# A fused convolution and feed-forward kernel on one core: five of the convolution's six sums moved from VectorE to accumulating transfers on GpSimd's queue

## The chip, the cores and the metric

The kernel runs on 1 core of one Trainium2 chip. The metric is the device time of one execution in microseconds (us), the median of several runs. The engines are named as the profile names them: PE is TensorE's matmul, PEld its weight load, DVE is VectorE, ACT is ScalarE, POOL is GpSimd, SP is SyncE; SPq and POOLq are the queues on which SP and POOL issue transfers. All durations below are from the profiler's record of one execution.

## The reference

A softmax over seven weights per position and head gives a causal convolution over the last seven positions, whose output goes through a two-layer network with a squared ReLU. The sizes are B = 8, S = 4096, D = 192, H = 8 heads, K = 7 taps, FF = 2048.

```python
w = np.exp(weight_gen - max over taps); w = w / (w.sum(-1, keepdims=True) + 1e-9)
x_unf = x_pad[:, idx, :].reshape(B, S, K, H, D // H)      # the last 7 positions
x = np.einsum('bshk,bskhg->bshg', w, x_unf).reshape(B * S, D)
r = np.maximum(x @ w_in, 0.0)
out = (r * r) @ w_out                                     # all float32
```

## The kernel before, in words

The 32768 rows lie as 256 rows on each of 128 partitions, and are worked through in 64 chunks of 512 rows (`TC = 4` rows on each partition, numbered `c` = 0 to 63). Each chunk goes through three stages.

**Convolution** (`conv_steps`): on DVE the softmax of the weights (six steps, lines 195 to 200, with one exponential on ACT), then for each of the seven taps a product `pr` of the input rows and the tap's weights (`mul(k)`, line 211, 128 x 768 floats), and six sums of products (`add(k)`, line 216). The sum goes through `turn` (line 270: a transpose in 32 x 32 blocks on DVE, then six transfers over a DRAM scratch `xd` on SP's queue into `xT`), and `split` (lines 235, 236) makes a high and a low part of it, `xh` on ACT and `xl` on DVE. Chunks 0 and 1 are turned on PE instead and have their own order of taps, which the change doesn't touch.

**First product** (`mm1`, line 300): eight steps `j` for each chunk; each makes two blocks `ph` of 128 of the 2048 hidden rows, with 18 matmuls. ACT then takes ReLU (`rg`, line 316), square (line 320) and a rounded high part `gh` (line 324); DVE takes the low part `gl = rg - gh` (line 328).

**Second product** (`mm2_turned`, line 372): 20 matmuls for each step, which read `gh` and `gl`. PE's order of work is written out: in step `j` of a chunk `mm1` of this step stands first and behind it `mm2` of the step that lies two steps back (`LAG = 2`). At the end of a chunk `sum_turned` (lines 380 to 383) and `store_turned` (lines 391 to 405) bring the output out, the latter with 24 small transfers and one large one on SP's queue. The input of two chunks is loaded together (`load_group`, lines 91 and 92), every second chunk.

The order on each engine is the order in which the program is written out (`manual_schedule`); the framework adds only the waits. The convolution of chunk `c + 2` is spread evenly over eight steps, from step 3 of chunk `c` to step 2 of chunk `c + 1`, by `spread`: element `i` of a list of `n` is put at step `3 + 8 * i // n`. Chunk 2 is an exception: its taps are spread over steps 0 to 3 of chunk 1. What is planned for a step stands on DVE behind the `gl` of the step before:

```python
for fb in fbs: relu(c, fb)
for fb in fbs: square(c, fb)
for f in late: f()                  # gl of the step before
if done is not None: sum_turned(done)
for f in todo.pop((c, j), []): f()  # the steps of the convolution
```

In the texts below "step 6" is `j` = 6, and the products, sums and transfers of a chunk bear the number of their tap: mul4 makes the product of tap 4. The buffers `pr` come from a pool; a product takes a buffer that the sum before has set free.

Of the kernel before, what the change touches and what calls it, by code (L numbers as in the profile page):

```python
# [8 lines left out]
F32 = mybir.dt.float32  # L9
# [3 lines left out]
ALU = mybir.AluOpType  # L13
# [6 lines left out]
def kernel(  # L20
# [9 lines left out]
    nc = tc.nc  # L30
    B, S, D = x.shape
    H, K = wg.shape[2], wg.shape[3]
    G = D // H
    FF = w_in.shape[1]
    P = 128
# [4 lines left out]
    TC = 4  # L40
# [19 lines left out]
    att = ctx.enter_context(tc.tile_pool(name="att", bufs=1))  # L60
# [121 lines left out]
    def conv_steps(c, on_pe):  # L182
        gi, lo = divmod(c, CPG)
        lo *= TC
        xt, wt = x_tiles[gi], w_tiles[gi]
        n = TC * H
        wf = wt[:, lo:lo + TC].rearrange("p t h k -> p (t h) k")
        mx = att.tile([P, n, 1], F32, name="mx", bufs=2)
        sm = att.tile([P, n, 1], F32, name="sm", bufs=2)
        sh = [P, n, K]  # L190
        parts = xts[c] = {}
        tt = nc.vector.tensor_tensor

        steps = [
            lambda: nc.vector.tensor_reduce(out=mx[:, :, 0], in_=wf, axis=AX.X, op=ALU.max),
            lambda: tt(out=wf, in0=wf, in1=mx.broadcast_to(sh), op=ALU.subtract),  # L196
            lambda: nc.scalar.activation(wf, wf, AF.Exp),  # L197
            lambda: nc.vector.tensor_reduce(out=sm[:, :, 0], in_=wf, axis=AX.X, op=ALU.add),
            lambda: (nc.vector.tensor_scalar_add(sm, sm, 1e-9), nc.vector.reciprocal(sm, sm)),
            lambda: tt(out=wf, in0=wf, in1=sm.broadcast_to(sh), op=ALU.mult),  # L200
        ]

        prs = {}

        def mul(k):
            def f():
                prs[k] = att.tile([P, TC, D], F32, name="pr", bufs=4)
                src = xt[:, lo + k:lo + k + TC, :].rearrange("p t (h g) -> p (t h) g", h=H)
                wk = wf[:, :, k:k + 1]
                dst = prs[k].rearrange("p t (h g) -> p (t h) g", h=H)  # L210
                tt(out=dst, in0=src, in1=wk.broadcast_to([P, n, G]), op=ALU.mult)  # L211
            return f

        def add(k, k0=0):
            def f():
                tt(out=prs[k0], in0=prs[k0], in1=prs.pop(k), op=ALU.add)  # L216
            return f

        def taps():
            fs = [mul(0), mul(1)]  # L220
            for k in range(1, K):
                if k + 1 < K:
                    fs.append(mul(k + 1))
                fs.append(add(k))
            return fs

        src = {}

        def split(k):
            def f():  # L230
                if k == 0:
                    parts["h"] = xtp.tile([P, ND, N], F32R, name="xh")
                    parts["l"] = xtp.tile([P, ND, N], F32R, name="xl")
                xh, xl = parts["h"][:, k], parts["l"][:, k]
                nc.scalar.copy(xh, src[k])  # L235
                tt(out=xl, in0=src[k], in1=xh.bitcast(F32), op=ALU.subtract)  # L236
            return f

        splits = [split(k) for k in range(ND)]

        if on_pe:
            def turn(k, first, last):
                def f():
                    if first:
                        for m in range(ND):
                            src[m] = ps_h.tile([P, N], F32, name="ph")
                    pr = prs.pop(k)
                    for m in range(ND):
                        for t in range(TC):
                            fl = dict(start=first and t == 0, stop=last and t == TC - 1)  # L250
                            x1 = pr[:, t, m * D1:(m + 1) * D1]
                            for h in range(2):
                                nc.tensor.matmul(src[m][h * D1:(h + 1) * D1, t * P:(t + 1) * P], x1, ident, **fl)  # L253
                return f

            if on_pe == 2:
                steps += [mul(6), mul(5), add(5, 6), turn(6, True, False),
                          mul(4), mul(3), add(3, 4), turn(4, False, False),
                          mul(2), mul(1), add(1, 2), mul(0), add(0, 2), turn(2, False, True)]
            else:  # L260
                steps += [mul(6), mul(5), add(5, 6), mul(4), add(4, 6), mul(3), add(3, 6), turn(6, True, False),
                          mul(2), mul(1), add(1, 2), mul(0), add(0, 2), turn(2, False, True)]
            return steps, splits

        def turn():
            xr = att.tile([P, D // Q, P], F32, name="xr")
            xT = att.tile([P, ND, N], F32, name="xT")
            for k in range(ND):
                src[k] = xT[:, k]
            nc.vector.transpose(  # L270
                xr.rearrange("p b (t j) -> p t b j", j=Q),
                prs.pop(0).rearrange("p t (b i) -> p t b i", i=Q),
            )
            xd = dram.tile([D, N], F32, name="xd")
            for q in range(P // Q):
                nc.sync.dma_start(
                    out=xd[:, q * P:(q + 1) * P].rearrange("(b i) n -> i b n", i=Q),
                    in_=xr[q * Q:(q + 1) * Q],
                )
            for h in range(2):  # L280
                nc.sync.dma_start(out=xT[h * D1:(h + 1) * D1], in_=xd.rearrange("(k p) n -> p k n", p=D1))

        return steps + taps() + [turn], splits


# [149 lines left out]
    load_rest()  # L435
    load_weights(2)
    sts, sp = conv_steps(0, 2)
    for f in sts[:10]:
        f()
# [12 lines left out]
    for u in range(NU):  # L452
# [18 lines left out]
        for _ in range((0, 0, 2, 2)[u]):  # L471
            square(0, sq)
            sq += 1
    load_group(1)
    conv1, split1 = conv_steps(1, 1)
    dec(NU + 1, 1, 2, 3, 4)
    for f in conv1[:6]:
# [16 lines left out]
    for f in conv1[13:]:  # L494
        f()
    conv2, split2 = conv_steps(2, 0)
    for f in conv2[:6]:
        f()
# [110 lines left out]
```

## Time and profile before

| | |
|---|---|
| time, median of 3 runs | 2247.62 us (2247.55 to 2247.77) |
| the profiled execution, first to last instruction | 2246.2 us, which is 1.4 us (0.06%) under the median of the runs |
| PE busy | 2228.7 us, 99% of the span |
| PEld busy | 1846.4 us, 82% |
| DVE busy | 1877.6 us, 84%, 2834 instructions |
| ACT busy | 1797.6 us, 80% |
| POOL busy | 1.7 us, 7 instructions, all at the start |
| DMA packets on SP's queue | 188.58 MB, 33.5% of 16 engines' span |
| granted TensorE clock | 1.000 over the whole run |

The table is read from the page's part 1 (busy time by engine), part 3 (DMA queues) and the view of the cores. A share of busy time is a mean over stages; what the work on an engine is worth is read from whether another engine waits for it. The profiled execution's own time is that of the span and of what lies outside it; the list of times does not say which of the runs it was, so the span is set against the median.

### The profile page before, as it was taken

What the parts mean: (1) busy time and instruction counts of PE and PEld (TensorE: products, weight loads), DVE (VectorE), ACT (ScalarE), POOL (GpSimd) and SP (SyncE); (2) the same over time, 40 slices, a digit from 0 to 9 for tenths busy, and PEclk for the clock granted to TensorE, in tenths of its full rate; (3) what the DMA queues carried; (4) which work ended last, traced back from release to release, by engine and by line L of the source; (5) the groups of instructions that cost most, each with busy time, mean ns of one, the idle gap of its engine ahead of it and who ended that gap; (6) DMA issues with size and microseconds to landing.
All of it is one profiled execution on the core that took longest, in us unless ns stands there. A gap on an engine that the chain in (4) does not pass through costs nothing.

```text
span 2246.2 us, 50242 instructions
## 1 busy us (share of the span) xinstructions
PE 2228.7 (99%) x19632; PEld 1846.4 (82%) x19632; DVE 1877.6 (84%) x2834; ACT 1797.6 (80%) x3462; POOL 1.7 (0%) x7
## 2 busy tenths in 40 slices
PE   7999999999999999999999999999999999999999
PEld 7788888888888888888888888888888888888887
DVE  8988888888888888888888888888888889888884
ACT  5688888888888888888888888888888888888876
POOL 0000000000000000000000000000000000000000
PEclk9999999999999999999999999999999999999999
DMA  5233233332333332333323333323333233332321
GB/s 170 60 91 90 58 99 85 91 100 67 80 94 81 100 88 59 99 84 93 99 54 93 88 88 99 83 65 100 84 91 90 57 99 86 91 99 71 76 66 45
DMA packets 321390, 191.78 MB, mean 85 GB/s; under 512 B 223752, under 2 KB 280968, under 8 KB 317184
## 3 DMA queue, kind: packets, MB, share of 16 engines
q1 hardware_dynamic: 321152, 188.58, 33.5%
q8 instruction: 153, 2.51, 0.5%
q14 instruction: 85, 0.70, 0.1%
HBM read 106.39 MB, written 49.55 MB: 69 GB/s over the span
## 4 chain that ended last, share of the span: by engine, by line
PE 97%; DVE 1%; ACT 1%; DMA 0%; issue 0%; SPq 0%; DVEq 0%; ACTq 0%
PE acc L372 49%; PE ph L300 45%; PE acc L336 1%; PE acc L345 1%; PE ph L253 1%; DVE pr L211 0%; DVE pr L216 0%; DMA xt<-in_x_dram 0%; ACT rg L320 0%; ACT gh L324 0%; DVE gl L328 0%; DMA raw<-in_moe_w_in_dram 0%; DVE V L156 0%; ACT rg L316 0%; ACT rg L310 0%
## 5 line engine op out<-in xcount | busy, mean ns | idle before, releaser
L372 PE MATMUL acc<-gh,V 64*128 64x512 f32 x5952 | 1007.5, 386 | 0.7 <-ACT gh L324 0.7
L300 PE MATMUL ph<-xh,W 64*128 64x512 f32 x6144 | 863.8, 386 | 2.0 <-ACT W L148 1.8
L316 ACT ACTIVATE rg<-ph 128x512 f32<-128x512 f32 x992 | 539.2, 597 | 346.9 <-PE ph L300 346.9
L372 PE MATMUL acc<-gl,V 64*128 64x512 f32 x3968 | 772.8, 386 | 1.0 <-DVE gl L328 1.0
L328 DVE TENSOR_TENSOR gl<-rg,gh 128x512 fp32r<-128x512 f32 x1008 | 644.4, 679 | 147.5 <-ACT gh L324 147.4
L300 PEld LDWEIGHTS ph<-xh,W 64*128 64x128 f32 x6144 | 575.8, 184 | 125.8 <-ACT W L148 3.0
L372 PEld LDWEIGHTS acc<-gh,V 64*128 64x128 f32 x5952 | 557.5, 184 | 118.1 <-ACT gh L324 1.1
L320 ACT ACTIVATE rg<-rg 128x512 f32<-128x512 f32 x1008 | 581.8, 634 | 0.0
L324 ACT CAST gh<-rg 128x512 fp32r<-128x512 f32 x1008 | 576.4, 627 | 2.6 <-PE acc L345 2.6
L372 PEld LDWEIGHTS acc<-gl,V 64*128 64x128 f32 x3968 | 371.7, 184 | 80.1 <-DVE gl L328 2.1
L300 PE MATMUL ph<-xl,W 64*128 64x512 f32 x3072 | 432.3, 386 | 0.0
L211 DVE TENSOR_TENSOR pr<-xt,wt 128x768 f32<-128x768 f32 x448 | 420.0, 950 | 3.4 <-DMA xt<-in_x_dram 1.2
L216 DVE TENSOR_TENSOR pr<-pr 128x768 f32<-128x768 f32 x381 | 361.5, 949 | 0.3
L300 PEld LDWEIGHTS ph<-xl,W 64*128 64x128 f32 x3072 | 288.3, 184 | 60.8 <-DVE xl L236 0.4
L236 DVE TENSOR_TENSOR xl<-xT,xh 128x512 fp32r<-128x512 f32 x186 | 117.7, 688 | 185.2 <-ACT xh L235 185.2
L235 ACT CAST xh<-xT 128x512 fp32r<-128x512 f32 x186 | 102.7, 625 | 0.0
L382 DVE TENSOR_TENSOR raw<-acc,raw 128x512 f32<-128x512 f32 x124 | 79.9, 686 | 3.0 <-ACT raw L380 3.0
L197 ACT ACTIVATE wt<-wt 128x224 f32<-128x224 f32 x64 | 25.0, 391 | 65.1 <-DVE wt L196 65.1
L380 ACT COPY raw<-acc 128x512 f32<-128x512 f32 x124 | 66.6, 598 | 0.0
L270 DVE STREAM_TRANSPOSE xr<-pr 128x768 f32<-128x768 f32 x62 | 60.7, 979 | 2.1
L394 DVE STREAM_TRANSPOSE raw<-raw 64x512 f32<-64x512 f32 x62 | 43.6, 704 | 2.1
L391 DVE STREAM_TRANSPOSE raw<-raw 128x512 f32<-128x512 f32 x62 | 43.7, 705 | 0.0
(46 smaller groups left out, 393.5 us busy)
## 6 DMA issues: line engine op xcount, KB each, us to landing
xT<-xd SPq DMA_DIRECT2D x124, 384.0 KB, 4.9
xt<-in_x_dram SPq DMA_DIRECT2D x31, 1344.0 KB, 7.0
out_dram<-o_sb SPq DMA_DIRECT2D x63, 384.0 KB, 2.7
xd<-xr SPq DMA_DIRECT2D x248, 96.0 KB, 2.0
o_sb<-raw SPq DMA_DIRECT2D x1488, 16.0 KB, 1.8
raw<-raw SPq DMA_DIRECT2D x62, 128.0 KB, 4.1
wt<-in_weight_gen_dram SPq DMA_DIRECT2D x31, 224.0 KB, 3.2
raw<-in_moe_w_in_dram SPq DMA_DIRECT2D x16, 192.0 KB, 4.1
```

The source lines that it names most:

```text
L211: tt(out=dst, in0=src, in1=wk.broadcast_to([P, n, G]), op=ALU.mult)
L216: tt(out=prs[k0], in0=prs[k0], in1=prs.pop(k), op=ALU.add)
L235: nc.scalar.copy(xh, src[k])
L236: tt(out=xl, in0=src[k], in1=xh.bitcast(F32), op=ALU.subtract)
L300: nc.tensor.matmul(two[i], w, xx[rows, k], start=(n == 0), stop=(n == len(seq) - 1))
L316: nc.scalar.activation(r, ph, AF.Relu)
L320: nc.scalar.activation(r, r, AF.Square)
L324: nc.scalar.copy(gh, rgs[c, fb])
L328: nc.vector.tensor_tensor(out=gl, in0=rgs.pop((c, fb)), in1=ghs[c, fb].bitcast(F32), op=ALU.subtract)
L372: nc.tensor.matmul(accs[c][b + h], w, g[rows], **fl)
L380: nc.scalar.copy(X[:, k], acc[b])
L382: nc.vector.tensor_tensor(out=X[:, k], in0=acc[b + 1], in1=X[:, k], op=ALU.add)
```

## The change

For the chunks 2 to 63 the list `taps()` is made in another way. All seven products stay on DVE. Five of the six sums are now transfers on GpSimd's queue, from one product buffer into another, which add what they bring to what is there (`accum_op=ALU.add`): products 1, 4 and 6 are added into the buffer of product 0, and products 3 and 5 into that of product 2. The sixth sum, buffer 2 into buffer 0, stays on DVE behind two empty places in the list. The pool `pr` has five buffers instead of four.

```diff
-                prs[k] = att.tile([P, TC, D], F32, name="pr", bufs=4)
+                prs[k] = att.tile([P, TC, D], F32, name="pr", bufs=5)
...
+        def moved(k, k0):
+            def f():
+                nc.gpsimd.dma_start(out=prs[k0], in_=prs.pop(k), accum_op=ALU.add)
+            return f
+
         def taps():
-            fs = [mul(0), mul(1)]
+            fs = [mul(0)]
             for k in range(1, K):
-                if k + 1 < K:
-                    fs.append(mul(k + 1))
-                fs.append(add(k))
-            return fs
+                fs.append(mul(k))
+                if k != 2:
+                    fs.append(moved(k, 0 if k in (1, 4, 6) else 2))
+            wait = [lambda: None] * 2
+            return fs + wait + [add(2)]
```

The list of a convolution has 22 places instead of 20 (six of the softmax, then seven products, five transfers, two empty places, one sum, the turn). By `3 + 8 * i // 22` they fall so: the softmax in steps 3 to 5, mul0, mul1 and the transfer of 1 in step 5; mul2 and mul3 in step 6; the transfer of 3, mul4 and the transfer of 4 in step 7; mul5, the transfer of 5 and mul6 in step 0 of the next chunk; the transfer of 6 in step 1; the sum and the turn in step 2. Line numbers behind line 217 move by 6: `gl` is line 334 after, `turn` line 276, `sum_turned` line 388, and the transfers are line 221.

DVE, in the middle of the run, from the `gl` at the head of step 7 on, before (`pr<-xt,wt` is a product, `pr<-pr` a sum, `raw<-acc` the output's sums in step 1; the names in brackets are the semaphores waited for, DMAHW of SP's transfers):

```order
L328 TENSOR_TENSOR gl<-rg,gh 128x512 [waits PE_49,Activation_49] x2
L211 TENSOR_TENSOR pr<-xt,wt 128x768
L216 TENSOR_TENSOR pr<-pr 128x768
L211 TENSOR_TENSOR pr<-xt,wt 128x768
L328 TENSOR_TENSOR gl<-rg,gh 128x512 [waits PE_49,Activation_49] x2
L216 TENSOR_TENSOR pr<-pr 128x768 [waits DVE_49]
L211 TENSOR_TENSOR pr<-xt,wt 128x768
L328 TENSOR_TENSOR gl<-rg,gh 128x512 [waits PE_49,Activation_49] x2
L382 TENSOR_TENSOR raw<-acc_3382,raw 128x512 [waits DMAHW2_49,DMAHW1_49,DMAHW3_49,DMAHW0_49,DMAHW6_49,PE_49,Activation_49]
L382 TENSOR_TENSOR raw<-acc_3380,raw 128x512 [waits PE_49,Activation_49]
L216 TENSOR_TENSOR pr<-pr 128x768 [waits DVE_49]
L211 TENSOR_TENSOR pr<-xt,wt 128x768
```

Behind these stand three more sums, the `gl` of step 1 and the transpose of the turn; no product or sum waits for a transfer here. The same place on DVE after, up to the turn (DMASW are the semaphores of GpSimd's transfers):

```order
L334 TENSOR_TENSOR gl<-rg,gh 128x512 [waits PE_49,Activation_49] x2
L211 TENSOR_TENSOR pr<-xt,wt 128x768
L334 TENSOR_TENSOR gl<-rg,gh 128x512 [waits PE_49,Activation_49] x2
L211 TENSOR_TENSOR pr<-xt,wt 128x768 [waits DMASW3_49]
L211 TENSOR_TENSOR pr<-xt,wt 128x768 [waits DMASW4_49]
L334 TENSOR_TENSOR gl<-rg,gh 128x512 [waits PE_49,Activation_49] x2
L388 TENSOR_TENSOR raw<-acc_3905,raw 128x512 [waits DMAHW3_49,DMAHW2_49,DMAHW4_49,DMAHW0_49,DMAHW5_49,PE_49,Activation_49]
L388 TENSOR_TENSOR raw<-acc_3903,raw 128x512 [waits PE_49,Activation_49]
L334 TENSOR_TENSOR gl<-rg,gh 128x512 [waits Activation_49] x2
L216 TENSOR_TENSOR pr<-pr 128x768 [waits DMASW7_49,DMASW6_49]
L276 STREAM_TRANSPOSE xr<-pr 128x4x6x32 [waits DMAHW4_49,DMAHW3_49,DMAHW5_49,DMAHW2_49,DVE_49]
```

The five sums are gone from the row. Mul5 now waits for the transfer of 1 (DMASW3) and mul6 for the transfer of 3 (DMASW4), whose buffers they take, and the one sum that is left waits for the transfers of 5 and 6 (DMASW6, DMASW7). GpSimd's queue, which held nothing here before, has for the same chunk:

```order
L221 DMA pr_4118<-pr_4120 128x768 [waits DVE_49]
L221 DMA pr_4204<-pr_4206 128x768 [waits DMASW4_49,DMASW2_49,DVE_49]
L221 DMA pr_4118<-pr_4274 128x768 [waits DMASW3_49,DVE_49]
L221 DMA pr_4204<-pr_4331 128x768 [waits DMASW4_49,DVE_49]
L221 DMA pr_4118<-pr_4334 128x768 [waits DMASW5_49,DVE_49]
```

These are the transfers of 1, 3, 4, 5 and 6, which count up DMASW3 to DMASW7. That of 4 waits for that of 1, that of 6 for that of 4, and that of 5 for that of 3, since each pair adds into one buffer. (The DMASW4 and DMASW2 of the second row were counted up for the chunk before.) SP's queue has the same transfers in the same order as before.

## The prediction

> **What bounds the kernel now.** I read the page's busy time first, then the view of waits by engine, then the order of time in one chunk in the middle, and last the transfers. The busy time by engine, and the granted TensorE clock in 40 slices:
>
> ```profile
> PE 2228.7 (99%) x19632; PEld 1846.4 (82%) x19632; DVE 1877.6 (84%) x2834; ACT 1797.6 (80%) x3462; POOL 1.7 (0%) x7
> PEclk9999999999999999999999999999999999999999
> ```
>
> All of PE's waits from 100 to 2240 us:
>
> ```profile
> PE acc L372 <- DVE gl L328: 0.4, 1, 0.4
> PE ph L300 <- ACT rg L310: 0.2, 1, 0.2
> ```
>
> PE is the bound, at full clock, and over 2140 us it waits for another engine 0.6 us in all. Three stretches of the view by windows (columns: length, then busy us and count of PE, PEld, DVE, ACT, POOL, the clock, DMA share, GB/s) show where PE has gaps:
>
> ```profile
> 56.00:100.00 44.00, 42.70 (x402) 35.44 (x402) 39.18 (x62) 27.81 (x58) 0.00 (x0) 1.00 0.24 73
> 100.00:112.00 12.00, 11.59 (x104) 9.25 (x102) 12.00 (x18) 10.33 (x21) 0.00 (x0) 1.00 0.06 12
> 1000.00:1035.00 35.00, 35.00 (x312) 28.94 (x310) 29.67 (x46) 28.53 (x56) 0.00 (x0) 1.00 0.28 62
> ```
>
> In the middle PE is busy 35.00 of 35 us while DVE has 5.3 us free. The changed stages have gaps only at the start: 44 - 42.70 + 12 - 11.59 = 1.7 us. So work taken off DVE can bring 1.7 us, 0.08%. The change can cost much more, if a wait for a transfer holds DVE until `gl` comes too late for PE.
>
> **What is removed.** The page's groups of products and sums:
>
> ```profile
> L211 DVE TENSOR_TENSOR pr<-xt,wt 128x768 f32<-128x768 f32 x448 | 420.0, 950 | 3.4 <-DMA xt<-in_x_dram 1.2
> L216 DVE TENSOR_TENSOR pr<-pr 128x768 f32<-128x768 f32 x381 | 361.5, 949 | 0.3
> ```
>
> 62 chunks by 5 sums by 0.949 us are 294 us of DVE, which would go from 1877.6 to 1583 us, 70% of the span. All of it lies beside PE's work, so it is worth 0 on the path, but for part of the 1.7 us. The products stay, and so does SP's order.
>
> **What is added: 310 transfers and three waits.** The trace has no adding transfer and none from GpSimd's queue. Their time from issue to landing, L, is the unknown of this case, and I first work out what L the order bears. DVE in the chunk at 1000 us, in order of time (start, length in us):
>
> ```profile
> 1009.65 0.95 DVE L216 TENSOR_TENSOR pr<-pr 128x768 f32<-128x768 f32 x1
> 1010.64 0.98 DVE L270 STREAM_TRANSPOSE xr<-pr 128x768 f32<-128x768 f32 x1
> 1011.54 1.25 DVE L328 TENSOR_TENSOR gl<-rg,gh 128x512 fp32r<-128x512 f32 x2
> ...
> 1028.89 0.95 DVE L216 TENSOR_TENSOR pr<-pr 128x768 f32<-128x768 f32 x1
> ...
> 1032.27 0.94 DVE L211 TENSOR_TENSOR pr<-xt,wt 128x768 f32<-128x768 f32 x1
> ```
>
> PE, one step of the same chunk:
>
> ```profile
> 1008.39 0.84 PE L300 MATMUL ph<-xh,W 64*128 64x512 f32 x6
> ...
> 1012.69 0.84 PE L300 MATMUL ph<-xh,W 64*128 64x512 f32 x6
> ...
> 1014.96 0.39 PE L372 MATMUL acc<-gl,V 64*128 64x512 f32 x2
> ```
>
> and ACT around the output's sums of step 1:
>
> ```profile
> 1038.47 1.08 ACT L380 COPY raw<-acc 128x512 f32<-128x512 f32 x2
> 1039.42 1.18 ACT L324 CAST gh<-rg 128x512 fp32r<-128x512 f32 x2
> ```
>
> A step of PE is 1012.69 - 1008.39 = 4.30 us, a chunk 8 x 4.305 = 34.44. The `gl` at 1011.54 are those of step 2, behind the turn; PE first reads them at 1014.96. One `gl` takes half of 1.25, some 0.65 us, so they may start at 1014.3 at the latest: 2.7 us to spare. A chunk later that is 1048.7.
>
> The chain after the change, with these durations: mul3 takes the place of the sum at 1028.89 and ends at 1029.84; mul4 takes that of the product at 1032.27 and ends at 1033.21. With the sums gone, the `gl` of step 7, mul5 and mul6 follow at once and mul6 ends near 1036.2 (1033.21 + 1.25 + 2 x 0.95 = 1036.4). The last sum has mul6, the `gl` of step 0 and the output's sums, which wait for ACT (1038.47 + 1.08), ahead of it, and the `gl` of step 1, whose `gh` is done at 1039.42 + 1.18 = 1040.6; DVE reaches it at about 1041.4. Sum and turn take 0.95 + 0.98, so the sum must start by 1048.7 - 1.9 = 1046.8 if PE isn't to wait. Three waits are to be met:
> - mul5 for the transfer of 1: mul1 stands in step 5, over 10 us ahead. Nothing.
> - mul6 for the transfer of 3, issued at 1029.84, needed at 1035.3: DVE idles if L is over 5.5 us. Behind it stands the `gl` of step 0, due for PE one step on, so that some 3 us more cost nothing.
> - the sum for the transfers of 4 and 6, one behind the other: mul4 ends at 1033.21, and both must have landed at 1046.8. 2 L <= 13.6, so L <= 6.8 us. The pair 3 and 5 starts 3.4 us earlier and has more. This is the wait that decides; past it each chunk loses 2 L - 13.6.
>
> Now L, by the nearest rows (KB each, median us to landing), and SP's row of the output's transfer within SBUF (shortest, median, longest):
>
> ```profile
> xT<-xd SPq DMA_DIRECT2D x124, 384.0 KB, 4.9
> xt<-in_x_dram SPq DMA_DIRECT2D x31, 1344.0 KB, 7.0
> out_dram<-o_sb SPq DMA_DIRECT2D x63, 384.0 KB, 2.7
> o_sb<-raw SPq DMA_DIRECT2D x1488, 16.0 KB, 1.8
> DMA to landing us min/median/max: 2.2/4.1/8.6
> ```
>
> An adding transfer of 128 x 768 floats brings 384 KB and must also read the 384 KB that it adds to. Below, 384 KB alone land in 2.7 us (`out`). Above, 1344 KB land in 7.0. Nearest is `xT`: two of 384 KB are issued together, 768 KB in 4.9 us. I take L = 4.9. Then the transfer of 3 lands at 1034.7 and mul6 doesn't wait; 4 lands at 1038.1, 6 at 1043.0; the sum starts there, 3.8 us ahead of its limit, and the turn ends at 1044.9, ahead of the 1010.64 + 34.44 + 0.98 = 1046.1 of before. Cost 0. If that cover is gone, a chunk pays what is over 13.6.
>
> **The load of every second chunk** lies across the transfer of 6:
>
> ```profile
> 1040.69 0.47 SPq L92 DMA_DIRECT2D xt<-in_x_dram  x1
> ...
> 1035.00:1037.00 2.00, 2.00 (x22) 1.65 (x20) 2.00 (x4) 0.85 (x3) 0.00 (x0) 1.00 0.20 33
> 1041.00:1043.00 2.00, 2.00 (x20) 1.66 (x18) 2.00 (x4) 2.00 (x5) 0.00 (x0) 1.00 1.13 331
> 1045.00:1047.00 2.00, 2.00 (x22) 1.65 (x20) 1.97 (x4) 1.92 (x4) 0.00 (x0) 1.00 0.84 311
> ```
>
> From 1041 to 1047 all DMA engines are taken (share about 1), against 0.20 before it. The transfer within SBUF issued in this burst lands in a median of 4.1 us instead of 2.2 at the shortest: 1.9 us more. For the transfer of 6 that makes 1044.9, still 1.9 ahead of 1046.8. PE is busy 2.00 of 2 us in and out of the burst, so traffic doesn't slow matmuls. The Trainium skill, "DMA: Bandwidth & Descriptors", section "Issuing engines are not separate DMA queues", states that all queues' transfers run on the same 16 engines and interleave; by that GpSimd's queue gives the transfer of 6 no way around the load, and I keep the 1.9 us.
>
> **Chunk 2**, whose taps are packed into four steps, has its own sum. DVE before, and ACT's exponential behind it:
>
> ```profile
> 68.71 2.69 DVE L211 TENSOR_TENSOR pr<-xt,wt 128x768 f32<-128x768 f32 x3
> 84.80 0.98 DVE L270 STREAM_TRANSPOSE xr<-pr 128x768 f32<-128x768 f32 x1
> 86.51 0.39 ACT L197 ACTIVATE wt<-wt 128x224 f32<-128x224 f32 x1 [6.08 <-DVE wt L196]
> ```
>
> After, mul3 and mul4 end near 73.4 and 74.3; mul6 waits for the transfer of 3 until 78.3 and ends at 79.2; the transfer of 6 lands at 84.1, and the turn starts at 85.1 instead of 84.80: 0.3 us later, with ACT's exponential and PE behind it. Against it stands the one wait for `gl` of some 0.3 us in this stage, whose `gl` come sooner. Sum 0.
>
> Sum: 2246.2 + 0 for the middle, 0 for chunk 2, 1.4 up to the median of the runs: 2247.6, and a few tenths for the start of a queue that wasn't used: 2248.
>
> A rule against the change is in the Trainium skill, "SBUF — State Buffer", section "Who interferes with whom": VectorE in a two-port mode shuts GpSimd out of SBUF, and transfers that GpSimd describes wait for it. If all DVE work held it so, each transfer would start up to 0.95 us later, L = 5.85, and the sum would still be 0; the page itself exempts TENSOR_TENSOR, nearly all that DVE runs here. No run before shows it.
>
> **Rivals.**
> (a) *L near 7, slower.* Adding costs more than reading 768 KB, as the 7.0 us of 1344 KB. A chunk loses 2 x 7.0 - 13.6 = 0.4 us, every second chunk 1.9 more in the burst, and chunk 2 some 5 us (2 x 2.1 more): 62 x 0.4 + 31 x 1.9 + 5 = 89 us, 2337. It decides from L = 5.9 on in the chunks with a load (2 x 5.9 + 1.9 = 13.7). For it: L is taken, not measured; GpSimd must make the descriptions itself. Against: no row of this size needs over 4.9 us outside the burst. Chance 0.20 for all between 2252.5 and 2340.
> (b) *L far above, slower by 10% and more.* At the longest landing within SBUF, 8.6 us: 2 x 8.6 - 13.6 = 3.6 us by 62 = 223, 2471. Or the DMA engines become the bound: 310 x 384 KB are 122 MB on top of 191.78 MB, twice that if the read of the target counts; 33.5% by (188.58 + 244) / 188.58 is 77%. That is room enough on the mean. Chance 0.13.
> (c) *Faster.* DVE's free time closes the gaps of the start: at most 1.7 us, 2246. Over 0.2% needs 4.5 us, which PE's waits don't hold. Chance 0.04.
>
> **How the numbers follow.** 0.2%, 4.5 us, is about what a measurement of this kernel can tell from no change. The forecast, no change, has 0.63 with its own range of 2246 to 2251; (a) 0.20, (b) 0.13, (c) 0.04. The range reaches from 2245 to the 2340 of (a) and leaves (b) and most of (c) out. Faster 0.04, same 0.63, slower 0.33.
>
> **What would show it.** The issues of the transfers have a landing time: under 5.9 us bears the forecast out, over 6.8 (a), over 8 (b). The sum's wait (L216 for DMA) should be about 1.6 us a chunk, mul6's none; DVE busy near 1583 us; PE's waits for `gl` as small as before. A wait of PE for DVE's `gl` of 0.4 us or more in each chunk would say that the chain of two transfers is too long; the same in every second chunk alone, that it was the load. The forecast is wrong if L is over 6.8 us, or if DVE slows down beside GpSimd's work.

## The result and the profile after

The changed kernel takes 2287.98 us (median of 4 runs, 2275.07 to 2292.80) against 2247.69 us before: 40.3 us longer, 1.8% by the medians; the ratio on record is 1.017 with an interval of 1.0151 to 1.0189. The stated range of 2245 to 2340 us held the time; the forecast, no change, did not. The profiled execution spans 2282.5 us, 36.3 more than before. The page after, in the lines that answer to those of before: busy time, the transfers' queues with their share of 16 engines (q1 is SP's, q0 GpSimd's), the groups of products and sums, and the transfers' landing times:

```profile
PE 2245.0 (98%) x19632; PEld 1872.9 (82%) x19632; DVE 1614.2 (71%) x2524; ACT 1797.8 (79%) x3462; POOL 268.5 (12%) x317
...
q1 hardware_dynamic: 321152, 188.58, 34.1%
q0 software_dynamic: 44640, 121.92, 30.2%
...
L211 DVE TENSOR_TENSOR pr<-xt,wt 128x768 f32<-128x768 f32 x448 | 409.8, 949 | 3.0 <-DMA pr<-pr 1.7
...
L216 DVE TENSOR_TENSOR pr<-pr 128x768 f32<-128x768 f32 x71 | 68.0, 958 | 103.8 <-DMA pr<-pr 103.4
...
pr<-pr POOLq DMA_DIRECT2D x310, 384.0 KB, 4.5
xT<-xd SPq DMA_DIRECT2D x124, 384.0 KB, 5.2
xt<-in_x_dram SPq DMA_DIRECT2D x31, 1344.0 KB, 7.6
out_dram<-o_sb SPq DMA_DIRECT2D x63, 384.0 KB, 2.7
xd<-xr SPq DMA_DIRECT2D x248, 96.0 KB, 3.2
o_sb<-raw SPq DMA_DIRECT2D x1488, 16.0 KB, 3.4
```

The adding transfers land in 4.5 us, near the 4.9 that I took; DVE is relieved; products take as long as before. But SP's small output transfers (`o_sb<-raw`) land in 3.4 us instead of 1.8. The view of waits (total us, times, longest) says what waited on the way to PE's work:

```profile
DVE pr L216 <- DMA pr<-pr: 103.4, 61, 3.8
ACT xh L241 <- DMA xT<-xd: 29.3, 18, 4.0
PE acc L378 <- DVE gl L334: 17.8, 14, 2.2
```

The sum waits 103.4 / 61 = 1.7 us a chunk, as worked out (1.6). It doesn't make the turn late: in the chunks with a load the turn's transpose starts 18.8 us behind the `xh` cast of the chunk before, against 19.5 us in the kernel before (medians). New is the second line: in 18 chunks ACT waits for xT, the turned sum that comes back over DRAM, and before there was no such wait. On the chain of work that ended last, transfers to xT hold 3% of the span.

The lost time can be placed by the first `xh` cast of each chunk on ACT. First and last of 62, before:

```profile
95.91 1.69 ACT L235 CAST xh<-xT 128x512 fp32r<-128x512 f32 x3
...
2196.97 1.66 ACT L235 CAST xh<-xT 128x512 fp32r<-128x512 f32 x3
```

and after:

```profile
97.46 1.66 ACT L241 CAST xh<-xT 128x512 fp32r<-128x512 f32 x3
...
2232.56 1.66 ACT L241 CAST xh<-xT 128x512 fp32r<-128x512 f32 x3
```

The 61 distances between them add up to 2101.06 us before and to 2135.10 us after, 34.0 us more. Every second one, behind a load of input, holds 32.4 of these; the others hold the rest. So I compared SP's queue in a chunk with a load, before and after (the load's `xt` row of before stands in the prediction):

```profile
1039.81 0.36 SPq L405 DMA_DIRECT2D out_dram<-o_sb  x1
...
1046.10 1.79 SPq L276 DMA_DIRECT2D xd<-xr  x4
1049.66 2.09 SPq L281 DMA_DIRECT2D xT<-xd  x2
```

```profile
987.39 0.36 SPq L411 DMA_DIRECT2D out_dram<-o_sb  x1
987.80 0.43 SPq L91 DMA_DIRECT2D wt<-in_weight_gen_dram  x1
988.27 0.47 SPq L92 DMA_DIRECT2D xt<-in_x_dram  x1
988.79 0.53 SPq L389 DMA_DIRECT2D raw<-raw  x1
989.36 3.04 SPq L282 DMA_DIRECT2D xd<-xr  x4
997.58 1.28 SPq L287 DMA_DIRECT2D xT<-xd  x2
```

The order is the same. Before, the load is issued 5.4 us ahead of the turn's first transfer and is nearly through when that comes; xT is issued 3.6 us after it. After, SP reaches the load only 1.1 us ahead of the turn, because it is held up by the small output transfers first; the turn's four transfers stand behind 1344 KB, and xT is issued 8.2 us after the first of them. Where that is too late, ACT waits, with DVE and PE behind it. In the worst chunk:

```profile
724.61 1.66 ACT L241 CAST xh<-xT 128x512 fp32r<-128x512 f32 x3 [3.96 <-DMA xT<-xd]
```
```profile
730.85 0.50 PE L378 MATMUL acc<-gl,V 64*128 64x512 f32 x2 [2.22 <-DVE gl L334]
```
```profile
730.00:735.00 5.00, 4.15 (x24) 3.32 (x26) 5.00 (x8) 3.40 (x7) 1.27 (x3) 0.69 0.78 136
```

After PE's wait of 2.22 us the granted clock (third number from the end of the window's row) is 0.69 over 5 us, so that this wait is paid for twice. Not every one is: of PE's six waits of 2.2 us, those that end at 731, 1567, 1782 and 1994 us are followed by 3.4 us at a clock of 0.50, those at 1640 and 2136 us are not. PE's busy time rose by 2245.0 - 2228.7 = 16.3 us though it does the same matmuls. Five such stretches of the clock, one of them chunk 2's, come to at most 5 x 3.4 x 0.5 = 8.5 us of that; in other stretches the matmuls follow each other more slowly at full clock, as behind the late `xh` above, where six of them show 1.54 us from 725.28 on instead of 0.84.

### The profile page after: what moved, and what is told of

The parts are those of the page before. It is cut to its first block, busy times and chain, and to the rows that moved or that the text cites. A ratio compares the mean times of both kernels' runs of the same rounds, so it can differ in the third digit from the quotient of the medians.

```text
span 2282.5 us, 50592 instructions
## 1 busy us (share of the span) xinstructions
PE 2245.0 (98%) x19632; PEld 1872.9 (82%) x19632; DVE 1614.2 (71%) x2524; ACT 1797.8 (79%) x3462; POOL 268.5 (12%) x317
## 3 DMA queue, kind: packets, MB, share of 16 engines
q1 hardware_dynamic: 321152, 188.58, 34.1%
q0 software_dynamic: 44640, 121.92, 30.2%
## 4 chain that ended last, share of the span: by engine, by line
PE 90%; DMA 4%; DVE 3%; ACT 2%; issue 1%; SPq 0%; DVEq 0%; ACTq 0%; POOL 0%; POOLq 0%
PE acc L378 46%; PE ph L306 42%; DMA xT<-xd 3%; DVE pr L211 1%; DVE xl L242 1%; PE acc L342 1%; PE acc L351 1%; PE ph L259 1%; ACT rg L322 1%; DVE gl L334 0%; ACT rg L326 0%; DMA pr<-pr 0%; ACT xh L241 0%; DVE raw L399 0%; DMA raw<-in_moe_w_in_dram 0%
## 5 line engine op out<-in xcount | busy, mean ns | idle before, releaser
L378 PE MATMUL acc<-gl,V 64*128 64x512 f32 x3968 | 782.2, 389 | 17.9 <-DVE gl L334 17.8
L306 PEld LDWEIGHTS ph<-xh,W 64*128 64x128 f32 x6144 | 585.2, 185 | 122.6 <-ACT xh L241 4.5
L378 PEld LDWEIGHTS acc<-gh,V 64*128 64x128 f32 x5952 | 566.4, 185 | 113.1 <-ACT gh L330 3.3
L221 POOL DMA_DIRECT2D pr<-pr x310 | 266.8, 861 | 1942.9 <-DVE pr L211 1694.0
L378 PEld LDWEIGHTS acc<-gl,V 64*128 64x128 f32 x3968 | 377.5, 185 | 99.1 <-DVE gl L334 25.7
L211 DVE TENSOR_TENSOR pr<-xt,wt 128x768 f32<-128x768 f32 x448 | 409.8, 949 | 3.0 <-DMA pr<-pr 1.7
L306 PEld LDWEIGHTS ph<-xl,W 64*128 64x128 f32 x3072 | 292.9, 185 | 59.1 <-DVE xl L242 2.1
L216 DVE TENSOR_TENSOR pr<-pr 128x768 f32<-128x768 f32 x71 | 68.0, 958 | 103.8 <-DMA pr<-pr 103.4
L241 ACT CAST xh<-xT 128x512 fp32r<-128x512 f32 x186 | 102.9, 622 | 29.7 <-DMA xT<-xd 29.3
```

What stands on the lines that cost most here:

```text
L221: nc.gpsimd.dma_start(out=prs[k0], in_=prs.pop(k), accum_op=ALU.add)
L306: nc.tensor.matmul(two[i], w, xx[rows, k], start=(n == 0), stop=(n == len(seq) - 1))
L378: nc.tensor.matmul(accs[c][b + h], w, g[rows], **fl)
```

## The experiments

My theory was: GpSimd's traffic makes the small transfers late. SP therefore issues the load late, right ahead of the turn's transfers, which stand behind it in SP's queue. The rivals were: the sum's new wait costs the time; or the traffic of all queues together is too much in any order.

**The load behind the turn.** In the changed kernel:

```diff
-            if j == 0 and c % 2 and (c + 3) // 2 * CPG < NCH:
+            if j == 4 and c % 2 and (c + 3) // 2 * CPG < NCH:
```

> The changed kernel, with the load of every second chunk (wt and xt) issued in step 4 instead of step 0, so that on SP's queue it stands behind the turn's six transfers and no longer ahead of them. Theory (queue order): in the changed kernel the 24 small output transfers land later beside GpSimd's traffic (median 3.4 us instead of 1.8), so SP reaches the load some 4.6 us later, right ahead of the turn's transfers, which then stand behind 1344 KB; xT comes late in the chunks with a load, and all of the 36 us are there. Then this edit gives the time of before: 2246 to 2252 us, no wait of ACT for xT, and the last sum still waits about 1.7 us a chunk for its transfer. Rival (the sum's new wait costs the time): unchanged, 2270 to 2293. Rival (the traffic of all queues together is too much, in whatever order): 2265 or more, with the lateness in other transfers.

Measured: 2251.48 us, ratio to before 1.0015 (1.0006 to 1.0025). The whole loss but 3.7 us is gone, with the same traffic. Its page and its waits of PE from 56 to 112 us:

```profile
xd<-xr SPq DMA_DIRECT2D x248, 96.0 KB, 2.1
o_sb<-raw SPq DMA_DIRECT2D x1488, 16.0 KB, 3.4
```
```profile
PE acc L378 <- ACT gh L330: 2.8, 1, 2.8
PE acc L378 <- DVE gl L334: 0.2, 1, 0.2
```

The small transfers are as late as in the changed kernel (3.4), the sum waits as long (105.8 us in all), and neither costs anything. From 112 us on PE waits 0.2 us in all; what is left lies in chunk 2's stage.

**The traffic alone.** In the kernel before, beside its six sums:

```diff
                 tt(out=dst, in0=src, in1=wk.broadcast_to([P, n, G]), op=ALU.mult)
+                if not on_pe and k in (1, 3, 4, 5, 6):
+                    nc.gpsimd.dma_start(out=extra, in_=prs[k], accum_op=ALU.add)
```

> The kernel before, with all six sums left on VectorE, and beside them five adding transfers of 384 KB for each chunk on GpSimd's queue, from products 1, 3, 4, 5 and 6 into one extra buffer that nothing reads: the traffic without the new wait of the sum and without the relief of VectorE. Theory (queue order): the traffic alone makes SP's small transfers late and the load with them, so the time goes up without any new wait on the path: 2252 to 2290 us, with ACT waiting for xT in the chunks with a load. Rival (the sum's new wait): the time of before, 2247.7. If the transfers come at moments that spare the small ones, the loss is at the low end.

Measured: 2330.38 us, ratio 1.0373 (1.0323 to 1.0423): more than I expected, with no sum waiting for a transfer.

```profile
ACT xh L237 <- DMA xT<-xd: 70.5, 30, 7.3
```

Here the five transfers follow each other into one buffer and reach into the turn: the last lands 9.3 us behind the start of the turn's transpose (in the changed kernel 1.1 us ahead of it), and the stretch from the first xd to xT is 9.3 us in the median. So this loss has a part that the changed kernel doesn't have, and its size doesn't carry over; SP's small transfers as a whole land in 2.1 us here, the last eight ahead of a load in 3.2 (medians). The sum's wait is ruled out as the cause, and so is the idea that a fuller DVE would have been safe.

**The control.** The later load of the first experiment, by the same edit, in the kernel before.

> The control: the kernel before with the same later load as the first run. Both theories: 2247.7, within 1 us; were it faster, the gain of the first run would not belong to the transfers.

Measured: 2247.85 us, ratio 1.0000 (0.9991 to 1.0010).

**Copies instead of additions.** In the changed kernel, the additions left out:

```diff
-                nc.gpsimd.dma_start(out=prs[k0], in_=prs.pop(k), accum_op=ALU.add)
+                nc.gpsimd.dma_start(out=prs[k0], in_=prs.pop(k))
```

> The changed kernel with its 310 transfers as plain copies from buffer to buffer: same queue, same waits, same bytes brought, but nothing is added, so the five sums are left out of the output. It tells what the adding costs. Theory (queue order): engines are taken for less time than the 30.2% of span by now (a plain 384 KB at the rate of SP's 188.58 MB for 34.1% would be 22%), L falls from 4.5 to some 3.5 us, the small transfers land sooner, and the loss shrinks to 0 to 25 us: 2248 to 2273. Rival (the sum's new wait): also less, since the chain of two is 2 us shorter. If L and the time stay as they are (2275 to 2293), adding costs nothing over copying.

Measured: 2247.45 us, ratio 0.9998 (0.9988 to 1.0008). Its queue and its landing time:

```profile
q0 software_dynamic: 24800, 121.92, 14.7%
```
```profile
pr<-pr POOLq DMA_DIRECT2D x310, 384.0 KB, 2.8
```

For the same bytes an addition takes the engines 2.1 times as long as a copy (30.2% of 2282.5 us against 14.7% of 2245.6), and lands 1.7 us later. With copies the small transfers land in 2.1 us, the load leads the turn by 2.3 us, and the sum hardly waits (7.2 us in all), so that the turn comes sooner: 16.9 us behind the `xh` cast of the chunk before, instead of 18.8. xT is issued 25.2 us behind that cast, instead of 28.8 (before: 24.2), and all of the loss is gone. I had expected part of it to stay. Copies relieve the queue and the sum at once, so this run does not say what each of the two is worth.

**Queue order without GpSimd.** In the kernel before, the load moved from its place at the head of a chunk into the turn, behind the first of its four transfers:

```diff
             for q in range(P // Q):
+                if q == 1 and c % 2 == 0 and c // 2 + 1 < NCH // CPG:
+                    load_group(c // 2 + 1)
                 nc.sync.dma_start(
```

> The kernel before, with no transfer on GpSimd's queue, and the load of every second chunk put on SP's queue behind the first of the turn's four transfers to xd, so that the other three and the two to xT stand behind it. Theory (queue order alone suffices): the turn's stretch from its first transfer to xT's issue grows from 3.6 us to 7 to 9 us as in the changed kernel (8.2), and eats the 5 us that xT has to spare: 2248 to 2275 us, in the chunks with a load only. Rival (the load alone is harmless, GpSimd's traffic has to slow it as well): 2247.8 and no wait for xT.

Measured: 2288.00 us, ratio 1.0175 (1.016 to 1.0191): the loss of the changed kernel, with POOL idle. I had put it lower.

```profile
ACT xh L235 <- DMA xT<-xd: 44.4, 30, 4.4
```

The granted clock fell only once here, in chunk 2's stage (mean 0.999), so the loss doesn't need a lower clock. A load at the wrong place of SP's queue suffices; GpSimd's part in the changed kernel is to bring it there.

**A longer chain.** In the first experiment's kernel the transfer of 6 three times:

```diff
-                nc.gpsimd.dma_start(out=prs[k0], in_=prs.pop(k), accum_op=ALU.add)
+                pr = prs.pop(k)
+                for _ in range(3 if k == 6 else 1):
+                    nc.gpsimd.dma_start(out=prs[k0], in_=pr, accum_op=ALU.add)
```

> The changed kernel with the later load, and the transfer of product 6 issued three times, one behind the other, into the same buffer, so that product 6 counts three times in the output. It tests the margin of 13.6 us from the end of mul4 to the last sum. In the changed kernel a transfer follows the one ahead of it after 3.9 us and lands 4.4 us after its issue, so the chain of four takes 3 x 3.9 + 4.4 = 16.1 us: 2.5 us too long a chunk, or 4.4 with the medians, by 62 chunks 155 to 270 us, and more where the clock falls after a wait: 2400 to 2560 us, with PE waiting for gl in every chunk. Rival (the margin is larger than I worked out): 2252, no waits of PE.

Measured: 2752.23 us, ratio 1.2244 (1.2222 to 1.2266), well above what I expected. PE's waits, and DVE at the end of mul4 and at the sum:

```profile
PE acc L380 <- DVE gl L336: 346.4, 61, 8.4
```
```profile
1006.88 0.94 DVE L211 TENSOR_TENSOR pr<-xt,wt 128x768 f32<-128x768 f32 x1
...
1027.63 0.96 DVE L216 TENSOR_TENSOR pr<-pr 128x768 f32<-128x768 f32 x1 [11.44 <-DMA pr<-pr]
```

From the end of mul4 (1007.82) to the sum the four transfers took 19.8 us (median of all chunks 19.5), not the 16.1 that I had counted: they follow each other after 5.1 us, not after 3.9, and already in the changed kernel the transfer of 6 follows that of 4 after 4.8 us (medians). Over the margin of 13.6 the chain above is 6.2 us too long; PE waits 346.4 / 61 = 5.7 a chunk. The margin holds to about half a microsecond, though only roughly, since PE's own steps are longer here. Of the rest of the 504 us, 11 are one wait of PE for chunk 2, and 147 lie in PE's busy time, 2376.3 us at a mean granted clock of 0.925.

**Chunk 2 as before**, in the first experiment's kernel:

```diff
         def taps():
+            if c == 2:
+                fs = [mul(0), mul(1)]
+                for k in range(1, K):
+                    if k + 1 < K:
+                        fs.append(mul(k + 1))
+                    fs.append(add(k))
+                return fs
             fs = [mul(0)]
```

> The changed kernel with the later load, and chunk 2 alone (whose taps are packed into four steps) with all its sums on VectorE as before. The first run's profile lost its 3 us between 56 and 112 us, where PE waits 2.83 us once for gh. Theory: that is chunk 2's chain of transfers, so this gives 2247.5 to 2248.2, the time of before. Rival (the rest of 3.7 us is spread over the run, from the traffic): 2251.

Measured: 2248.12 us, ratio 1.0002 (0.9993 to 1.0010). So 2251.48 - 2248.12 = 3.4 us were chunk 2's.

**Chunk 2 mixed**, the one version that could have beaten both kernels:

```diff
         def taps():
+            if c == 2:
+                nop = lambda: None
+                return [mul(0), mul(1), moved(1, 0), mul(2), mul(3), moved(3, 2), mul(4), nop,
+                        mul(5), add(5, 4), mul(6), add(6, 4), nop, add(4), add(2)]
             fs = [mul(0)]
```

> As the run before, but chunk 2 has two transfers (1 into 0, 3 into 2) with nothing chained behind them, and four sums on VectorE. Theory: the two sums taken off VectorE in the one stage where it is full close part of PE's 1.7 us of gaps there: 2246.0 to 2247.6. It is the version that could beat both kernels, by 0.1% at most. Rival: a wait for the transfer of 3 takes it back, 2247.8 or more.

Measured: 2248.20 us, ratio 1.0002 (0.9993 to 1.0011): no gain. PE's busy time between 56 and 112 us rose by 0.3 us (54.59 against 54.28), too little to be seen in the time.

**An earlier load, ahead of the output.** In the changed kernel the load moved up by one place of SP's queue:

```diff
-            if j == 0 and c % 2 and (c + 3) // 2 * CPG < NCH:
+            if j == 0 and c == 1:
...
+        if part and c % 2 and (c + 5) // 2 * CPG < NCH:
+            load_group((c + 5) // 2)
         if part:
             nc.sync.dma_start(out=out_v[:, c * TC:(c + 1) * TC, :], in_=o_sb)
```

> The changed kernel with one thing moved: on SP's queue the load of every second chunk stands just ahead of the output's large transfer, which waits for the small ones to land, and no longer behind it. SP issues the last small transfer some 4 us before the large one (983.5 against 987.4 us in one chunk of the changed kernel), so the load gets a lead of about 4 to 5 us on the turn instead of 0.55. Theory (SP's wait for the small transfers makes the load late, and the lead sets the loss): the turn's stretch falls from 8.2 to 4 to 6 us, most of the 33 us of the chunks with a load go, and what stays is chunk 2's 3 to 4 us: 2250 to 2258. Rival (the lead doesn't matter, GpSimd's traffic slows the load by itself): 2275 or more.

Measured: 2251.14 us, ratio 1.0016 (1.0007 to 1.0026). The lead is less than I expected (3.05 us) and the stretch longer (6.6), but hardly any waiting for xT is left:

```profile
ACT xh L241 <- DMA xT<-xd: 0.2, 1, 0.2
```

So a lead of some 3 us is enough here, and SP's wait for the landing of the small transfers is a part of what takes the lead away. The traces show the other part: in the chunks with a load SP issues the last of the 24 small transfers 14.6 us behind the `xh` cast of the chunk before, against 11.7 us in the kernel before, since 250 of all 1488 issues hold SP's queue for over 1.2 us instead of the usual 0.6 (51 before). From there to its landing is 3.5 us instead of 2.0, and the load is issued at 19.2 us instead of 15.0 (medians). This run takes only the wait for the landing away, and the load goes out at 16.7 us.

Over the chunks with a load (29 of each trace, medians from SP's order of time; lead: from the issue of `xt` to the end of the turn's transpose; stretch: from the first xd to xT's issue; ACT's wait for xT is the total in the trace):

| kernel | lead us | stretch us | ACT's wait for xT us | time us |
|---|---|---|---|---|
| before | 5.6 | 3.6 | 0 | 2247.7 |
| changed | 0.55 | 8.2 | 29.3 | 2288.0 |
| load behind the turn | behind it | 3.6 | 0 | 2251.5 |
| load ahead of the output | 3.05 | 6.6 | 0.2 | 2251.1 |
| copies | 2.3 | 7.3 | 0 | 2247.5 |
| before, traffic alone | 2.2 | 9.3 | 70.5 | 2330.4 |
| before, load in the turn | -0.9 | 8.9 | 44.4 | 2288.0 |

The lead alone doesn't set the loss. Copies and the traffic alone have nearly the same lead, but with copies the turn comes sooner, and with the traffic alone an addition lies across it.

## Why the prediction was right in part, and wrong in its forecast

The time lies in the stated range because the range reached up to rival (a), whose mechanism did not come. That is luck, and bears out neither the forecast nor (a).

- **PE is the bound, and relief of DVE is worth nothing:** right. With the load moved and chunk 2 as before, DVE is as free as in the changed kernel and the time is that of before within 0.3 us. DVE's busy time fell by 263 us, not 294: the next instruction starts some 0.87 us behind the start of a sum, so that 0.949 counts part of the time twice.
- **L = 4.9 us, two transfers within 13.6 us, the sum's wait:** right in what they say, 4.5 us and 1.7 us a chunk; mul6 waited 1.7 us in the whole run. That the wait comes out so well is partly luck: two landings of 4.5 us alone would give 0.8. The 0.3 us from the end of mul4 to the first issue and the 0.6 us between the first landing and the second issue, which the sum had at nothing, make up for L. (The 1036.2 that stands beside its own sum, 1036.4, changes nothing.) The longer chain bears the margin out to about half a microsecond.
- **"The products stay, and so does SP's order", costed at nothing:** this is the step that failed. SP's order did stay; its times did not. I weighed what the load does to GpSimd's transfer, and not what GpSimd's transfers do to SP's queue. The cover to name was the 5.4 us by which the load went ahead of the turn; with 1.1 us left of it, the chunks with a load lose 32 us. The trace of before has the small transfers whose landing SP waits for (`SPq L405 <- DMA o_sb<-raw`, 76.4 us among the waits of SP's queue), and the sum doesn't use them.
- **The load of every second chunk:** the right chunks, the wrong victim. The transfer of 6 was to be late; it was the turn. Of the signs that I named, L over 6.8 us and a slower DVE did not come, though the forecast was wrong; PE's waits for `gl` (17.8 us in 14 waits) did, and the load is what they pointed to.
- **Chunk 2, 0:** too small. The turn was to start at 85.1 us and PE's loss to be made up; it started at 86.07, PE waited 2.9 us at once, and the stage cost 3.4 us.
- **"A few tenths for the start of a queue that wasn't used":** no run shows this term. With GpSimd's queue in use the times without a loss are 2248.12 us (chunk 2 as before) and 2247.45 us (copies), around the 2247.81 us of before.
- **Rival (a)** had the sign, a size of the right order (89 us) and every second chunk, but by a wait of the sum at L near 7, which didn't come. That the DMA engines fill up, in (b), was nearer to the cause: they are taken for 34.1 + 30.2 = 64% on the mean, which is no bound, but SP's small transfers land later beside the additions. The output's large transfer doesn't (2.7 us in both).
- **The Trainium skill**, "SBUF — State Buffer", "Who interferes with whom": products took 949 ns after against 950 before, and GpSimd's issues took 0.86 us both where DVE was busy for over 90% of them (197) and where it was for under 10% (18), so nothing speaks for an exclusion of either engine. That the page gives TENSOR_TENSOR no two-port mode, and infers that it doesn't hold up the describing of transfers, agrees with the trace.
- **The Trainium skill**, "DMA: Bandwidth & Descriptors", "Issuing engines are not separate DMA queues": the trace agrees, 1.8 to 3.4 us for SP's small transfers beside GpSimd's. I had used it in one direction only, for what SP's load does to GpSimd's transfer.

What stays open: why the chunks with a load lose between 0 and 4.1 us each in the changed kernel, and why SP's small transfers are issued and land more slowly. That a small transfer waits within the engines behind the parts of an addition fits the copies' 2.1 us against 3.4, but was not shown by itself.

## What to carry to other kernels

Before moving work to another queue, ask not only who waits for the new transfers, but which transfers of the other queues will land later, which queue waits for those, and what stands in that queue behind the thing that gets late. Such a shift is a term of its own in the sum, with a cover in microseconds and a price if the cover goes. A large load that nobody needs soon belongs behind the short transfers that somebody waits for, or far ahead of them, and never by chance right in front. And an engine that is 84% busy is worth nothing to relieve, as DVE here, if the one that bounds the kernel never waits for it.

## What the runs showed of the hardware

- An adding transfer within SBUF of 128 x 768 floats took 2.1 times the engine time of a copy of the same bytes (30.2% of 2282.5 us against 14.7% of 2245.6 us for 310), landed in 4.5 against 2.8 us, and held GpSimd's queue for 861 ns at its issue against 539 ns.
- Beside additions, transfers of 16 KB on another queue went from 1.8 to 3.4 us in the median, beside copies to 2.1. Beside the same number of additions at other moments (the traffic alone) they went to 2.1 too.
- Behind four of six waits of PE of 2.2 us the granted clock was 0.50 for 3.4 us; behind the other two it stayed at 1.00. The Trainium skill, "TensorE: Matmul & The Clock Gate", "Why this matters for your kernels", asks for no idle gaps over some 3 us; here shorter ones were enough in four cases of six.
